# Retention attention in chunks of 64 positions, with the two batches of a pair in the two halves of the partitions

## The chip, the core and the metric

The kernel runs on one core of a Trainium2 chip. The core has a matrix engine (TensorE, "PE" in the profile, with its loads of the stationary operand counted apart as "PEld"), three engines for elementwise work (VectorE "DVE", ScalarE "ACT", GpSimd "POOL") and a fifth, SyncE "SP", that here only starts transfers. Each engine works through its own list of instructions in order. SP, ACT and POOL start DMA transfers from their lists too, and such an instruction stands in the engine's queue like any other. TensorE writes to PSUM, which has eight banks of 512 f32 in each of the 128 partitions; DVE and ACT read PSUM, POOL does not.

The metric is the device time of the program in microseconds, the median of several runs. A change of more than about 0.2% can be told from none.

## The reference

A retention layer without softmax feeds a multiplicative feed-forward layer. With 8 batches, 8 heads, 576 positions and 64 values per head, all f32:

```python
scores = q @ k.T / sqrt(64)                # per batch and head, 576 x 576
rel    = pos[:, None] - pos[None, :]
Dmat   = where(rel >= 0, gamma[h] ** rel, 0)
x      = (scores * Dmat) @ v               # put back as 4608 tokens x 512
a, b   = x @ w1, x @ w2                    # each 4608 x 1024
out    = (a * b @ w3) @ w_out              # 4608 x 512
```

The weights come as 64-bit floats and are turned into f32 on the chip.

## The kernel before

**Attention.** `gamma ** rel` is split: q is multiplied by `gamma ** pos` and v by `gamma ** -pos`, so the mask is only a triangle of ones. The sequence of a pair of batches is cut into five chunks, the first of 64 positions and four of 128; a pair and a chunk are one group g, 20 in all (`NC` = 5 chunks, `G` = 20; groups 0, 5, 10 and 15 are the short ones). Positions lie in the partitions of the loaded tiles `ld_k`, `ld_q`, `ld_v`, with 16 batch-and-head columns of 64 values beside one another. For each group there are four stages on TensorE, each with 16 small matmuls (every f32 matmul shows as two loads and two matmuls in the profile, so that a stage is 32 of each):

- `score` (L233): k times q, contracted over 64 values, a 128 by 128 result. Two of them stand in the array at once, in its two row halves. The results fill four PSUM banks `sc`, and four DVE multiplications by the mask (L236) write them to `pm`.
- `state` (L255): k times v, contracted over 128 positions, added up over the chunks in one PSUM bank `st`. Two at once, in the two column halves. ACT copies the sum to `sb` (L259).
- `pv_state` (L274): the state before the chunk times q. Contraction and output are both 64 wide: four at once, one in each quarter of the array.
- `pv` (L299): `pm` times v, contracted over 128 positions, two at once in the column halves, added to the same two banks `xps`; ACT copies them to `xT` (L306).

q and k must stand with the 64 values in the partitions before `score`. In some groups PE transposes them (`front`, L218, copied by ACT at L221), in others they are loaded in blocks of 32 by 32 (`load_blocks`, L171, 16 transfers a tile on SP's queue) and transposed by DVE (L190). v is scaled by POOL or DVE (L204), or by eight ACT instructions, one a head for both batches (L202).

**Feed-forward.** The large products use Strassen's scheme. Up to about 157 us `up` (L524) multiplies tokens by w1 and w2 while DVE and ACT convert the weights; up to 212 us w3 is multiplied by w_out (L477); then `down` (L637), and from 363 us on `up2` (L1028), a second form with seven steps a half. One `up2` step is seven products of four matmuls (0.65 us each): p1, p5, the product left over from the step before, then one onto a bank that ACT first filled with p1 (`seed`, L1047), then three more. Its weights come back from DRAM into a ring of three places (`ra`, L939 on POOL's queue).

**Order.** The order of all instructions is written out by hand. In the last part the loop over groups runs some `up2` and `down` steps by `work(n)`, then `pv(g)` with its copies, then the load of v for group g+2 (L93, on POOL's queue), `state(g+1)` and `score(g+1)`. The load of v waits until `pv(g)` has read the buffer. The ACT scaling of that v is put into the list `beside` and is issued in two halves in the first two `up2` steps after it (L1058); where the group has only `down` steps, it is issued after them, just before `pv`. The transposes of the next q and k on DVE are put into `aside`, in the last two steps before `pv`.

**Banks.** All results but `st` and the two `seed` banks are allotted in turn from a pool `acc`, of seven banks up to 335 us and of five from then on (L925): each new tile takes the bank used longest ago and waits until that one has been read. In the last part these are p1 and p5 of every `up2` step, five results of every `down`, and `xps` (two) and `sc` (four) of each group.

Of the kernel before, what the change touches and what calls it, by code (L numbers as in the profile page):

```python
# [8 lines left out]
F32 = mybir.dt.float32  # L9
# [10 lines left out]
def kernel(  # L20
# [31 lines left out]
    G = NB2 * NC  # L52
    NB = 3
# [27 lines left out]
    acc = acc_part.enter_context(tc.tile_pool(name="acc", bufs=7, space=PSUM))  # L81
# [5 lines left out]
    def load(g, names, engine=nc.sync):  # L87
        i, c = divmod(g, NC)
        sz = sizes[c]
        src = {"k": k, "q": q, "v": v}  # L90
        for nm in names:
            t = pools["ld"].tile([P, 2 * H, D], F32, tag="ld_" + nm, name="ld_" + nm)
            engine.dma_start(  # L93
                t[:sz], src[nm][2 * i:2 * i + 2, :, starts[c]:starts[c] + sz, :].rearrange("b h p d -> p (b h) d"))
            live[nm, g] = t

    dq = ffn.tile([P, 4, 2, TB], F32, tag="c", name="dq", bufs=1).rearrange("p a b s -> p (a b s)")[:H, :S]
    nc.scalar.dma_start(dq, decay_q)
# [8 lines left out]
                            base=0, pattern=[[1, P]], channel_multiplier=-1)  # L107

# [3 lines left out]
    gk = const.tile([P, NC, H], F32, tag="gk", name="gk")  # L112
    gq = const.tile([P, NC, H], F32, tag="gq", name="gq")
    gqs = const.tile([P, NP, S // 32], F32, tag="gqs", name="gqs")
    nc.scalar.dma_start(gk[:short, 0, :], decay_k[:short, :])
    nc.scalar.dma_start(gk[:, 1:, :], decay_k[short:, :].rearrange("(c p) h -> p c h", p=P))
# [3 lines left out]
    gps = acc.tile([P, NC, H], F32, tag="acc", name="gps")  # L120
    for c in range(NC):
        nc.tensor.transpose(gps[:sizes[c], c, :], dq[:, starts[c]:starts[c] + sizes[c]], ident[:H, :H])
    for c in (0, slice(1, NC)):
        n = short if c == 0 else P
        nc.vector.tensor_copy(gq[:n, c, :], gps[:n, c, :])
# [69 lines left out]
    def scale(g, nm, scalar=False, engine=nc.gpsimd):  # L195
        c = g % NC
        sz = sizes[c]
        t, gam = live[nm, g], {"q": gq, "v": gk}[nm]
        t = t[:sz].rearrange("p (b h) d -> p b h d", b=2)
        if scalar:  # L200
            for h in range(H) if scalar is True else scalar:
                nc.scalar.mul(t[:, :, h, :], t[:, :, h, :], gam[:sz, c, h:h + 1])  # L202
            return
        engine.tensor_tensor(  # L204
            out=t, in0=t, in1=gam[:sz, c].unsqueeze(1).unsqueeze(3).to_broadcast([sz, 2, H, D]), op=ALU.mult)

    def front(g, names="kq"):
        c = g % NC
        sz = sizes[c]
        for nm in names:  # L210
# [3 lines left out]
            for b in range(2):  # L214
                tp = acc.tile([P, NP, P], F32, tag="acc", name="tp")
                for p in range(NP):
                    h = b * H + 2 * p
                    nc.tensor.transpose(tp[:, p, :sz],  # L218
                                        src[:sz, h:h + 2, :].rearrange("p a d -> p (a d)"),
                                        ident[:sz, :sz])  # L220
                nc.scalar.copy(dst[:, b, :, :sz], tp[:, :, :sz])  # L221
            live[nm + "T", g] = dst

    def score(g):
        c = g % NC
        sz = sizes[c]
        kT, qT = live["kT", g], live["qT", g]
        pm = pools["fr"].tile([P, 2, 2, NP, P], F32, tag="pm", name="pm", bufs=1)
        for b in range(2):
            sc = [acc.tile([P, NP, P], F32, tag="acc", name="sc") for j in range(2)]  # L230
            for p in range(NP):
                for j, hs in enumerate(heads):
                    nc.tensor.matmul(sc[j][:sz, p, :sz], kT[hs, b, p, :sz], qT[hs, b, p, :sz],  # L233
                                     start=True, stop=True)
            for j in range(2):
                nc.vector.tensor_mul(pm[:sz, b, j, :, :sz], sc[j][:sz, :, :sz],  # L236
                                     mask[:sz, :sz].unsqueeze(1).to_broadcast([sz, NP, sz]))
        live["pm", g] = pm

    def state(g):  # L240
        c = g % NC
        sz = sizes[c]
        if c == NC - 1:
            return
        vs = live["v", g]
        kn = live["k", g]
        if c == 0:
            live["st"] = st_ps.tile([P, 2, NP, D], F32, tag="st", name="st")
        st = live["st"]

        for b in range(2):
            for p in range(NP):
                for j, hs in enumerate(heads):
                    h = b * H + 2 * p + j
                    nc.tensor.matmul(st[hs, b, p, :], kn[:sz, h, :], vs[:sz, h, :],  # L255
                                     start=(c == 0 and b == 0 and p == 0), stop=(c == NC - 2),
                                     skip_group_check=True)
        sb = pools["fr"].tile([P, 2, NP, D], F32, tag="sb", name="sb")
        nc.scalar.copy(sb, st)  # L259
        live["sb", g + 1] = sb  # L260

    bank_order = [(b, n) for b in range(2) for n in range(2)]

    def pv_state(g):

        sz = sizes[g % NC]
        qT = live["qT", g]

        banks = live["xps", g] = [acc.tile([P, 2, 2, P], F32, tag="acc", name="xps") for r in range(2)]
        if g % NC:  # L270
            for m, (b, n) in enumerate(bank_order):
                for r, j in ((0, 0), (0, 1), (1, 0), (1, 1)):
                    p = 2 * r + n
                    nc.tensor.matmul(banks[r][heads[j ^ r], b, n, :sz], live["sb", g][heads[j], b, p, :],  # L274
                                     qT[heads[j], b, p, :sz], start=(m == 0), stop=False,
                                     skip_group_check=True)

    def pv(g):
# [16 lines left out]
        for m, (b, n) in enumerate(bank_order):  # L295
            for r in range(2):
                for half in range(2):
                    p, j = 2 * r + n, half ^ r
                    nc.tensor.matmul(banks[r][heads[half], b, n, :sz], vs[:sz, b * H + 2 * p + j, :],  # L299
                                     pm[:sz, b, j, p, :sz], start=(c == 0 and m == 0), stop=True,  # L300
                                     skip_group_check=True)
# [425 lines left out]
    state(0)  # L727
# [14 lines left out]
    pv_state(1)  # L742
    convert_up_to(3)
    convert(2)
    state(1)
# [19 lines left out]
    state(2)  # L765
# [5 lines left out]
    copies = pv(2)  # L771
# [4 lines left out]
    state(3)  # L776
# [8 lines left out]
    pv(3)()  # L785
# [4 lines left out]
    owed.append(2)  # L790
    pv(4)()
# [129 lines left out]
    def open_second():  # L921
# [3 lines left out]
        acc = ctx.enter_context(tc.tile_pool(name="acc", bufs=5, space=PSUM, reuse_waits="tile"))  # L925
# [198 lines left out]
    state(NC)  # L1124
# [4 lines left out]
    for g in first_pair:  # L1129
# [21 lines left out]
        pv(g)()  # L1151
        load(g + 2, "v", nc.scalar if in_blocks[g + 2] else nc.sync)
        if in_blocks[g + 2] and (g + 2) % NC != NC - 1:
            load(g + 2, "k")
        state(g + 1)
        score(g + 1)
# [35 lines left out]
    state(g)  # L1192
# [3 lines left out]
    for g in range(2 * NC, G):  # L1196
# [27 lines left out]
        pv(g)()  # L1224
# [3 lines left out]
        if g + 2 < G:  # L1228
            load(g + 2, "v", nc.gpsimd)
            if (g + 2) % NC != NC - 1:  # L1230
                loads.append(lambda g=g: load(g + 2, "k", nc.gpsimd))
        if g + 1 < G:
            state(g + 1)
            score(g + 1)
# [49 lines left out]
```

## Time and profile before

| | |
|---|---|
| median of 3 runs | 858.88 us (858.45 to 860.29) |
| the profiled execution | 850.68 us, its span 848.9 us |
| mean granted TensorE clock | 0.989 |
| PE busy | 819.3 us (97%), 6085 matmuls |
| DVE, POOL, ACT busy | 541.2, 325.6, 283.2 us |
| DMA | 126.96 MB, mean 150 GB/s |

The groups' attention falls into three stretches: 0 to 83 us (groups 0 to 4), 231 to 340 us (5 to 9) and 385 to 706 us (10 to 19; the score of group 10 is at 364 us). Their mean busy times, by the view of windows:

| stretch, us | PE | DVE | ACT | POOL | DMA share | GB/s |
|---|---|---|---|---|---|---|
| 0 to 83 | 73.81 | 64.88 | 58.27 | 6.64 | 0.93 | 195 |
| 231 to 340 | 107.31 | 63.31 | 15.27 | 33.05 | 0.61 | 150 |
| 385 to 706 | 315.24 | 197.62 | 101.62 | 185.58 | 0.62 | 167 |

A line of the profile names the kernel's line, the engine, what is written and what is read; "x32" is a count of instructions, and "<-" ahead of a time in brackets names what ended the engine's wait. In the chain of waits each piece has its start, its length and what it was. Times of one profiled execution are all measured from its first instruction.

### The profile page before, as it was taken

The numbers are of one execution on the slowest core, as the hardware profiler recorded it, in microseconds if no ns is written. First come the engines' busy times: TensorE is split into PE (matmuls) and PEld (weight loads), VectorE is DVE, ScalarE is ACT, GpSimd is POOL, SyncE is SP. The second block draws the span as 40 slices with busy tenths as digits, with TensorE's granted clock in tenths as the row PEclk, the third lists the DMA queues.
The fourth block names the chain that finished last, engine by engine and source line by source line (L and its number), as shares of the span: only waits on it lengthen the run. The fifth ranks groups of instructions, "written<-read, shape, count | busy, mean of one in ns | idle before, by whom it ended". The sixth has DMA issues, their size and how long they took to land.

```text
span 848.9 us, 15774 instructions
## 1 busy us (share of the span) xinstructions
PE 819.3 (97%) x6085; PEld 738.1 (87%) x6085; DVE 541.2 (64%) x887; ACT 283.2 (33%) x581; POOL 325.6 (38%) x330
## 2 busy tenths in 40 slices
PE   7899999999999999979998999999999999999998
PEld 6889999644989998869998889998899998899987
DVE  4899999991644477615657644759735768446653
ACT  4777556670111101033343024342034331033300
POOL 1100010001104181395545935556916468445500
PEclk8999999999999999999999999999999999999999
DMA  9995454436046487979786147787275452245401
GB/s 193 217 224 128 77 150 125 126 98 112 1 98 125 75 220 251 307 209 220 190 229 167 44 93 228 201 238 177 58 156 183 140 208 69 77 148 189 159 25 51
DMA packets 201291, 126.96 MB, mean 150 GB/s; under 512 B 161272, under 2 KB 183032, under 8 KB 201216
## 3 DMA queue, kind: packets, MB, share of 16 engines
q1 hardware_dynamic: 170944, 50.14, 29.1%
q0 software_dynamic: 11776, 63.71, 23.0%
q10 hardware_dynamic: 18496, 12.10, 5.3%
q8 instruction: 48, 0.79, 0.4%
q14 instruction: 27, 0.22, 0.1%
HBM read 103.62 MB, written 22.28 MB: 148 GB/s over the span
## 4 chain that ended last, share of the span: by engine, by line
PE 79%; DMA 7%; DVE 7%; issue 3%; SPq 2%; ACT 1%; POOL 0%; ACTq 0%; DVEq 0%; POOLq 0%
PE po L637 24%; PE up L1028 15%; PE up L524 13%; PE seed L1028 11%; PE ps L477 6%; DMA ld_v<-in_v_dram 3%; PE xps L299 3%; PE sc L233 3%; DMA ra<-kept 2%; PE xps L274 1%; SPq L171 1%; DVE c L529 1%; DVE ab L1003 1%; DMA bl_q<-in_q_dram 1%; PE st L255 1%
## 5 line engine op out<-in xcount | busy, mean ns | idle before, releaser
L637 PE MATMUL po<-w3o,ab 128*128 128x256 f32 x552 | 125.0, 381 | 1.4 <-DVE ot L641 0.5
L637 PEld LDWEIGHTS po<-w3o,ab 128*128 128x128 f32 x552 | 103.9, 190 | 17.4 <-DVE ot L641 1.2
L1033 POOL TENSOR_TENSOR cc<-cc 128x384 f32<-128x384 f32 x112 | 109.3, 1001 | 4.1 <-ACT cc L1051 2.4
L1040 DVE TENSOR_TENSOR cc<-seed,cc 128x384 f32<-128x384 f32 x88 | 48.7, 553 | 72.9 <-PE seed L1028 68.5
L181 POOL TENSOR_TENSOR bl_q<-bl_q,gqs 128x512 f32<-128x512 f32 (+1 forms) x30 | 30.8, 1048 | 127.7 <-DMA bl_q<-in_q_dram 91.8
L939 POOL DMA_DIRECT2D ra<-kept x54 | 30.6, 567 | 124.1 <-PE seed L1028 103.3
L1028 PE MATMUL up<-xT,ra 128*128 128x192 f32 x384 | 74.2, 330 | 0.6 <-DMA ra<-kept 0.6
L1040 DVE TENSOR_TENSOR cc<-up,cc 128x384 f32<-128x384 f32 x88 | 48.4, 550 | 36.8 <-PE up L1028 31.5
L524 PE MATMUL up<-xT,wA 128*128 128x192 f32 x384 | 70.4, 327 | 0.0
L529 DVE TENSOR_TENSOR c<-up,c 128x384 f32<-128x384 f32 x80 | 44.0, 550 | 38.9 <-PE up L524 38.3
L1028 PEld LDWEIGHTS up<-xT,ra 128*128 128x128 f32 x384 | 64.4, 192 | 2.0 <-DMA ra<-kept 0.9
L236 DVE TENSOR_TENSOR pm<-sc,mask 128x512 f32<-128x512 f32 (+1 forms) x80 | 45.4, 626 | 32.1 <-PE sc L233 32.0
L637 PE MATMUL po<-wB,forms 128*128 128x256 f32 x288 | 65.2, 379 | 0.5 <-DVE forms L611 0.5
L524 PEld LDWEIGHTS up<-xT,wA 128*128 128x128 f32 x384 | 63.4, 190 | 1.1 <-issue 0.5
L637 PEld LDWEIGHTS po<-wB,forms 128*128 128x128 f32 x288 | 54.6, 190 | 8.2 <-PE po L637 0.8
L1047 ACT COPY seed<-up 128x384 f32<-128x384 f32 x56 | 25.9, 463 | 100.1 <-PE up L1028 46.6
L1028 PE MATMUL seed<-e,ra 128*128 128x192 f32 x256 | 52.9, 337 | 5.2 <-DVE cc L1040 2.9
L1028 PE MATMUL up<-ra 128*128 128x192 f32 x288 | 55.1, 328 | 1.9 <-DMA ra<-kept 1.9
L477 PE MATMUL ps<-wo,w3T 128*128 128x512 f32 x128 | 55.1, 592 | 0.0
L204 POOL TENSOR_TENSOR ld_v<-ld_v,gk 128x1024 f32<-128x1024 f32 (+1 forms) x9 | 17.1, 1899 | 90.5 <-DMA ld_v<-in_v_dram 90.5
L679 DVE TENSOR_TENSOR ab<-ab,forms 128x512 f32<-128x512 f32 x17 | 17.1, 1008 | 53.3 <-PE po L637 53.3
L1028 PEld LDWEIGHTS seed<-e,ra 128*128 128x128 f32 x256 | 43.7, 194 | 7.8 <-DVE cc L1040 3.6
(127 smaller groups left out, 1597.2 us busy)
## 6 DMA issues: line engine op xcount, KB each, us to landing
ra<-kept POOLq DMA_DIRECT2D x54, 896.0 KB, 5.0
raw<-in_moe_w_dram SPq DMA_DIRECT2D x72, 128.0 KB, 3.0
bl_q<-in_q_dram SPq DMA_DIRECT2D x216, 32.0 KB, 3.2
out_dram<-ot ACTq DMA_DIRECT2D x54, 128.0 KB, 2.3
bl_k<-in_k_dram SPq DMA_DIRECT2D x136, 32.0 KB, 2.4
raw<-in_moe_w_dram SPq DMA_DIRECT2D x16, 256.0 KB, 6.0
ld_k<-in_k_dram SPq DMA_DIRECT2D x8, 512.0 KB, 5.9
raw<-in_moe_w_out_dram SPq DMA_DIRECT2D x32, 128.0 KB, 2.7
```

Of the source, the lines that this page charges most:

```text
L181: nc.gpsimd.tensor_tensor(out=part, in0=part, in1=gqs[:, :, n0:n0 + n].unsqueeze(3).to_broadcast([P, NP, n, BL]), op=ALU.mult)
L233: nc.tensor.matmul(sc[j][:sz, p, :sz], kT[hs, b, p, :sz], qT[hs, b, p, :sz], start=True, stop=True)
L236: nc.vector.tensor_mul(pm[:sz, b, j, :, :sz], sc[j][:sz, :, :sz], mask[:sz, :sz].unsqueeze(1).to_broadcast([sz, NP, sz]))
L477: nc.tensor.matmul(ps, live["w3T", ft][:, g, :], live["wo"][:, g, :], start=(g == 0), stop=(g == KF - 1))
L524: nc.tensor.matmul(ps[:, w, :], a[:, w, r, :], b[:, r, :], start=(new and w == r == 0), stop=(w == r == 1), skip_group_check=True)
L529: nc.vector.tensor_add(c[:, to], ps, c[:, sb])
L637: nc.tensor.matmul(ps[nm], a[A][:, f, :], live["W"][B][:, f, :], start=(f == 0 and not on), stop=(f == NP - 1), skip_group_check=True)
L939: engine.dma_start(ring[n % 3], kept[n % 14 // 7][nm])
L1028: nc.tensor.matmul(ps[:, w, :], weight_of(slot, a, w), B[b], start=(new and w == 0), stop=True, skip_group_check=True)
L1033: nc.gpsimd.tensor_tensor(out=o, in0=o, in1=i, op=ALU.add)
L1040: nc.vector.tensor_add(c[:, j], ps, with_add[:, j])
L1047: nc.scalar.copy(p6, p1)
```

## The change

A chunk of 64 positions takes the place of the 128, but a group keeps its 64 or 128 positions: it has one or two chunks (`chunks(g)`), and a loaded tile now holds batch 0 of the pair in partitions 0 to 63 and batch 1 in 64 to 127, with a chunk index s, 8 heads and 64 values in the free dimension. Every matmul of the four stages has 64 rows, 64 columns and 64 moving columns, and four of them stand in the four quarters of the array.

- `score`: 32 matmuls a full group into two `sc` banks, two mask multiplications in place of four; `pm` has two buffers of half the size.
- `state(g, s)`: 16 matmuls and one ACT copy for each chunk; `st` takes two banks, so `acc` has six and later four.
- `pv_state`: 16 matmuls a chunk, with the state of that chunk.
- `pv`: in two halves (`second`); between them ACT reads one column of a bank into `hand`, and the second half waits for that. Callers pass work to be put between the halves: `state(g, 1)` and `score(g + 1)`, which ran after `pv` before.
- `load`: two transfers a chunk (one a batch), four in place of one for a full group; in the last chunk of a pair k is loaded for the first 64 positions, as `state(g, 0)` needs them.
- `scale` on ACT: one instruction a head and chunk, 16 in place of 8 for a full group.

The core of it:

```diff
-    acc = acc_part.enter_context(tc.tile_pool(name="acc", bufs=7, space=PSUM))
+    acc = acc_part.enter_context(tc.tile_pool(name="acc", bufs=6, space=PSUM))
...
-            t = pools["ld"].tile([P, 2 * H, D], F32, tag="ld_" + nm, name="ld_" + nm)
-            engine.dma_start(
-                t[:sz], src[nm][2 * i:2 * i + 2, :, starts[c]:starts[c] + sz, :].rearrange("b h p d -> p (b h) d"))
+            t = pools["ld"].tile([P, 2, H, D], F32, tag="ld_" + nm, name="ld_" + nm)
+            for s in range(n):
+                s0 = starts[c] + s * CS
+                for b in range(2):
+                    engine.dma_start(t[heads[b], s], src[nm][2 * i + b, :, s0:s0 + CS, :].rearrange("h p d -> p h d"))
...
             for h in range(H) if scalar is True else scalar:
-                nc.scalar.mul(t[:, :, h, :], t[:, :, h, :], gam[:sz, c, h:h + 1])
+                for s in range(n):
+                    nc.scalar.mul(t[:, s, h, :], t[:, s, h, :], gam[:, n0 + s, h:h + 1])
...
+        sc = [acc.tile([P, 2, NP, CS], F32, tag="acc", name="sc") for j in range(2)]
+        for s in range(n):
+            at_s = slice(s * CS, (s + 1) * CS)
             for p in range(NP):
+                for b in range(2):
+                    for j, hs in enumerate(heads):
+                        nc.tensor.matmul(sc[j][heads[b], s, p, :], kT[hs, b, p, at_s], qT[hs, b, p, at_s],
+                                         start=True, stop=True)
...
+        for p in range(NP):
+            for b, rows in enumerate(heads):
                 for j, hs in enumerate(heads):
+                    h = 2 * p + j
+                    nc.tensor.matmul(st[hs, b, p, :], kn[rows, s, h, :], vs[rows, s, h, :],
+                                     start=(g % NC == 0 and p == 0), stop=at_end, skip_group_check=True)
...
+        for second in range(2):
+            if second:
+                nc.scalar.copy(hand[heads[0]], banks[1][heads[0], 1, 1, sz - 1:sz])
+                for work_between in fill:
+                    work_between()
+            for s in range(chunks(g)):
+                for n in range(2):
+                    for b, half in ((0, 0), (1, 1), (0, 1), (1, 0)):
+                        r = b ^ half ^ second
+                        p, j = 2 * r + n, half ^ r
+                        nc.tensor.matmul(
+                            banks[r][heads[half], b, n, s * CS:(s + 1) * CS], vs[heads[b], s, 2 * p + j, :],
+                            pm[heads[b], j, s, p, :], start=(c == 0 and not second and n == 0), stop=True,
+                            skip_group_check=True)
...
-        acc = ctx.enter_context(tc.tile_pool(name="acc", bufs=5, space=PSUM, reuse_waits="tile"))
+        acc = ctx.enter_context(tc.tile_pool(name="acc", bufs=4, space=PSUM, reuse_waits="tile"))
...
-        pv(g)()
+        if g + 1 < G:
+            pv(g, lambda: state(g, 1), lambda: score(g + 1))()
+        else:
+            pv(g)()
...
-            state(g + 1)
-            score(g + 1)
+            state(g + 1, 0)
```

Groups 0, 1, 4, 9 and 19 have nothing between the halves of `pv`; groups 2 and 3 have `state(g, 1)` alone. The tables of decays are laid out by 64 positions, which takes one more transfer of q's decays.

## The prediction

> **What bounds the kernel now.** The page first:
>
> ```profile
> span 848.9 us, 15774 instructions
> PE 819.3 (97%) x6085; PEld 738.1 (87%) x6085; DVE 541.2 (64%) x887; ACT 283.2 (33%) x581; POOL 325.6 (38%) x330
> PE 79%; DMA 7%; DVE 7%; issue 3%; SPq 2%; ACT 1%; POOL 0%; ACTq 0%; DVEq 0%; POOLq 0%
> ```
>
> PE is the bound: the chain lies on it for 79% of the span. So the first question is what the four stages cost it, which the chain of waits shows in one late group (11):
>
> ```profile
> 414.01 1.03 PE xps L274 x32
> 415.05 1.90 PE xps L299 x32
> 416.94 0.93 PE st L255 x32
> 417.88 1.99 PE sc L233 x32
> 419.86 1.50 PE up L1028 x8
> ```
>
> 5.85 us a full group. L274 has four matmuls at once (8 turns of 0.129), L299 two of the same 128 columns (16 turns of 0.119), L255 two of 64 columns (16 turns of 0.058). So four at once cost a turn no more than two, and half the columns halve it.
>
> The second question is what stands ready to take PE's place. ACT's and POOL's timelines behind the same group:
>
> ```profile
> 416.77 1.07 ACT L306 COPY xT<-xps 128x512 f32<-128x512 f32 x2 [4.12 <-PE xps L299]
> 417.92 0.59 ACT L259 COPY sb<-st 128x512 f32<-128x512 f32 x1
> 423.69 1.28 ACT L202 ACTIVATE ld_v<-ld_v,gk 128x128 f32<-128x128 f32 x4 [0.47 <-DMA ld_v<-in_v_dram]
> 424.88 0.46 ACT L1042 COPY cc<-up 128x384 f32<-128x384 f32 x1
> 425.29 0.46 ACT L1047 COPY seed<-up 128x384 f32<-128x384 f32 x1
> ...
> 417.87 1.21 POOL L93 DMA_DIRECT2D ld_v<-in_v_dram  x1 [3.62 <-PE xps L299]
> ```
>
> The load of v starts when `pv` has ended (416.78) and lands 5.8 us later. ACT waits for it, scales, and only then fills the bank (L1047) for a product of the next step, which PE reaches at 426.39: 0.6 spare. Behind group 14 nothing is spare, and the chain leaves PE altogether:
>
> ```profile
> 508.70 6.37 DMA ld_v<-in_v_dram
> 515.10 0.92 ACT ld_v L202 x3
> 516.28 0.46 ACT cc L1042
> 516.74 0.39 ACT seed L1047
> 517.17 0.92 PE seed L1028 x4
> ```
>
> Third, how late DVE is when a group starts (group 18, PE there at 664.2):
>
> ```profile
> 662.23 2.74 DVE L1003 TENSOR_TENSOR ab<-cc 128x384 f32<-128x384 f32 x1
> 664.90 1.23 DVE L190 STREAM_TRANSPOSE kT<-bl_k 128x1024 f32<-128x1024 f32 x1
> 666.97 0.54 DVE L1040 TENSOR_TENSOR cc<-up,cc 128x384 f32<-128x384 f32 x1
> 667.89 0.53 DVE L1040 TENSOR_TENSOR cc<-up,cc 128x384 f32<-128x384 f32 x1
> ```
>
> The last two free the banks of p1 and p5, at 667.5 and 668.4. With five `acc` banks the first `sc` tile has a free bank; with four, the two `sc` tiles need just these two.
>
> **The change part by part.**
>
> *The array.* Each stage of a full group becomes 16 turns of four matmuls of 64 columns: at 0.058, 0.93 us. Four stages 3.73, and 0.2 for entering the mode once (1.03 against 8 turns of 0.109 shows 0.16): 3.9 against 5.85, 1.9 us saved. Over 16 full groups, and some 1.1 in the four short ones, about 35 us of PE time. The turn isn't in the trace: bounded below by 0.058 (L255), above by 0.129 (L274, were its 128 columns no part of the price), which makes 8.25 a group. I take 0.058, as both halvings have a row.
>
> [...]
>
> *What PE meets after the stages.* The next product takes the first `xps` bank, whose copy (0.59) starts when `pv` ends, with only `state(g+1, 0)` (0.47) between: 0.3 lost. So 1.6 of the 1.9 at best, work starting 4.25 after the group's start in place of 5.85.
>
> *`hand`.* The copy is tiny, but PE's whole queue stands behind it. Group 11 has 1.4 us of fill, which covers a copy and two semaphores (0.5, L306's row starts 0.1 after its matmul). Without cover (groups 0, 1, 4, 9, 19) it costs 0.5. It stands in ACT's queue behind the scaling: in group 17 that runs 626.06 to 628.51 as eight, so to about 630.0 as sixteen.
>
> *ACT's scaling.* Sixteen of 64 for eight of 128. L202 takes 0.295 (four in 1.28); copies of 256 and 512 (0.37, 0.59) give 0.84 ns an element, so 0.24 each and a batch of eight 2.0 in place of 1.28: 0.75 later.
>
> *The load of v.* `pv` now ends with `state(g, 1)` and `score(g + 1)` inside it: at start + 3.4 in place of 2.85, 0.55 later. Four transfers for one: POOL's short load takes 0.86, so issue is at most 3.4 in place of 1.21 (+2.2); a short load lands 4.5 after issue against 6.4 (down to -1.5). I take the landing as unchanged, between the two. So L1047 is 0.55 + 0.75 = 1.3 later than before, and PE, 1.6 earlier, waits for it: the gain is gone, and 1.3 less the spare time is lost.
>
> *Four banks.* Where DVE is late (groups 13, 15, 16, 18), `score(g + 1)`, now in the middle of `pv`, waits for p5's bank or kT, and `pv`, `xT` and the load of v behind it.
>
> *DVE* loses 40 of 80 mask multiplications (about 0.62: 25 us), beside PE; nothing on the path, as what makes it late stands ahead of them. *Second state copies*: 16 x 0.59 on ACT, read a group later; nothing, with ACT at 33%; 0.6 each if ACT were late. *k of last chunks*: four loads of 256 KB beside 0.62 DMA share; nothing. *k loads on POOL*: up to +2.2 us of issue in each of six groups, ahead of POOL's ring loads and L1033; up to 1 each if DVE waits for these (it spends 5.4 us waiting for L1033 now); nothing taken. *More instructions to fetch*: nothing, PE's loads and matmuls doubled in these stages only. *`acc` at six*: `up` needs a bank back after 2.6 us, ACT returns it in time; nothing.
>
> **By stretch** (+ is time won):
>
> 0 to 83 us (DMA share 0.93, ACT 58 of 83): the chain runs through loads and their issues on SP, where a blocked issue takes 2.66 and 6.59 us, which absorbs most of some 40 more issues; PE's savings don't count, and in group 1 the `hand` copy stands behind the conversion's ACT work. -1.0 (from -5 to +3).
>
> 231 to 340 us: ACT and POOL are light. Group 5 +0.5 and +2.0; group 6 nothing, since kT for group 8 waits for SP's 33 issues (266.8 to 285.9), counted from the transposes of group 7; group 7 +1.8; group 8 +0.9 (no state before); group 9 +0.3. Sum +5.5 (from +2 to +8).
>
> 385 to 706 us, by the terms above:
> - 10: kT's copy (391.2) holds `score`, `pv` ends 0.95 later, 0.75 for ACT, 0.5 spare, 0.2 of the wait hidden: -1.0.
> - 11: -1.3 + 0.6, so -0.6. 12: ACT, not the load, led there, with 1 spare: 0.
> - 13: kT at 465.2 as before; the left-over product now comes after `score`, and its three DVE multiplications hold the next `down`: -1.0.
> - 14: `pv` ends 0.2 later, 0.75 for ACT, nothing spare: -1.0.
> - 15: `score` waits until 547.1, so `pv` ends at 548.4 in place of 543.9: v lands at 555.2, L1047 done at 558.1 in place of 554.2; -3.4, of which the 0.8 us that PE now waits at 561.8 for `ra` is taken up: -2.8.
> - 16: `score` waits until 585.5, the left-over product comes 2.5 later, its multiplications hold `down`: -0.7.
> - 17: `hand` waits for the scaling, `pv` ends 2.1 later, 0.75 for ACT: between -1.6 and -2.9; -2.0.
> - 18: `score` at 668.5, work at 670.9 in place of 669.8: -1.1.
> - 19: +0.3.
>
> Sum -9.9. In all -1.0 + 5.5 - 9.9 = -5.4. The profiled execution's 850.7 (span 848.9 and 1.8 around it) would become 856.1. It lies 8.2 under the median, so the forecast against the median is 858.9 + 5.4, 864.
>
> **Rivals.**
>
> *The gain is kept.* If the four smaller loads land about 1.5 us sooner (the short load's row), ACT is no longer late behind 10, 11, 12, 14 and 17: +1.5, +1.6, +1.6, +1.1, +1.6, with 0.3 for 19 and nothing for the late-DVE groups, +7.7; with +5.5 and 0 at the start, 13.2 faster: 845. For it: the short load's row. Against it: POOL must issue four. It decides the sign when more than about 1 us of landing is won in each.
>
> *Issue binds.* The four issues on POOL take 3.4, and the last part lands 2 us later; behind 10, 11, 12, 14, 15 and 17 that goes straight into the chain, 6 x 2.0: 876. For it: the 0.86 row; against it: parts move while others are issued.
>
> *The turns don't shrink.* At 0.129 a group costs 8.25 + 0.2: 2.4 x 16 = 38 us more, 897. For it: no row has four at once with 64 columns. Against it: both halvings in the rows.
>
> **How the numbers follow.** The main case 0.50, gain kept 0.28, issue 0.13, turns 0.09. The main case's own range is 858 to 871, from the ends of its stretches (-5 + 2 - 13 to +3 + 8 - 8, pulled in since they don't fall together). Leaving out the turns (0.09) and the lower part of the kept gain (0.10) gives 845 to 877. No change (within 0.2%, 1.7 us, what a measurement here can tell): 0.10, from between the main case and the kept gain; faster 0.30; slower 0.60, the rest.
>
> **What would show it.** Each stage at 0.93 for 64 matmuls in the chain (over 1.5: the turns). L202 in batches of eight near 2.0, starting on the DMA, and PE's first `seed` product of the second `up2` step waiting about 2 us for L1047, in groups 10, 11, 14, 15, 17. PE waiting in `score` for L1040 or kT in 13, 15, 16, 18. `pv`'s second half in 17 waiting for ACT. In the middle stretch PE time falls by about 8 and the end moves by about 5. The prediction is wrong if L202 finds v there (then it is faster), or if the ring loads on POOL come late (then slower).

## The result and the profile after

The changed kernel takes 915.69 us against 858.66 us: 1.066 times as long, with an interval of 1.057 to 1.074. Measured once more beside later experiments it was 1.073 times (1.062 to 1.084). The forecast was 864 us, with 877 as the upper end: the sign was right, and some 50 us were missing. The profiled execution took 916.36 us. Runs of one and the same kernel spread more than the 0.2% named at the start: those of the kernel before went from 846 to 860 us beside the experiments, so the intervals are what a difference is to be judged by.

The page of the changed kernel, the lines that answer to those of before, and the row of the queue that brings instructions (blocks, MB, share of the 16 DMA engines; it had 48 blocks before):

```profile
span 914.6 us, 20159 instructions
PE 811.1 (89%) x8121; PEld 727.3 (80%) x8121; DVE 536.7 (59%) x847; ACT 309.9 (34%) x709; POOL 345.5 (38%) x372
q8 instruction: 64, 1.05, 0.5%
PE 60%; DMA 13%; DVE 9%; SPq 5%; issue 5%; POOL 4%; ACT 4%; ACTq 0%; DVEq 0%; POOLq 0%
```

TensorE is no longer the whole story: its share of the chain fell from 79% to 60%, and everything else on the chain grew. Two sums over the starts of all matmuls say by how much. A matmul's own time is taken as the time to the next start, but no more than its columns need; the rest is waiting. Own time fell from 788.1 to 764.1 us, waiting rose from 55.6 to 145.4 us; -24.0 and +89.8 make the +65.7 of the two spans.

Not all of this waiting is standing still. The mean granted clock of TensorE fell from 0.989 to 0.963. By the view of windows it was 0.50 from 448.8 to 452.2 us, at the end of the stop shown below and behind it, and from 500.0 to 503.4 us, behind a wait of 4.4 us for `kT`, where the 64 matmuls of `score` took 1.99 us in place of 0.93. If what was withheld always came as a half, as it did there, the two means amount to 68 us at half speed in place of 19. By the same sums, matmuls that took up to twice their time in such stretches make about 13 of the 89.8 us (an estimate). This comes behind the waits; no experiment here takes it apart from them.

Group 11 shows the gain and its end. The chain of waits (start, length, what):

```profile
443.52 1.09 PE xps L282 x64
444.61 0.47 PE xps L315 x32
445.07 0.47 PE st L261 x32
445.54 0.93 PE sc L237 x64
446.48 0.11 PE xps L315 x6
446.58 2.43 issue
449.02 1.01 PE xps L315 x25
```

Here the stages are as fast as forecast: 64 matmuls in 0.93 to 1.09 us. Then, in the middle of `pv`'s second half, TensorE stands still for 2.43 us, and the profile names nothing that it waits for. The stop alone is more than the 1.9 us that the group was to win. The waits of TensorE over the whole span (us in total, times, longest) have more of that kind, and others:

```profile
PE seed L1048 <- ACT seed L1067: 9.7, 5, 5.4
PE xps L315 <- ACT hand L307: 9.7, 8, 2.7
PE po L654 <- DVE forms L628: 8.6, 2, 7.1
...
PE sc L237 <- issue: 7.6, 2, 5.1
PE sc L237 <- DVE cc L1060: 7.3, 6, 2.9
PE xps L315 <- issue: 4.9, 3, 2.4
...
PE sc L237 <- DVE kT L198: 4.4, 1, 4.4
PE st L261 <- issue: 4.1, 3, 1.9
```

Before, the row with the most had 3.0 us in all.

Where the time was lost is seen by comparing when the same product of `up` or `up2` runs. How much later than before it is, in us, in the profiled executions of the changed kernel and of some of the experiments below:

```
product, at us in the kernel before     91.8  283.7  315.7  399.6  455.1  529.0  649.3  759.1
the changed kernel                      17.7   17.8   19.5   27.7   34.7   49.6   57.8   65.8
changed, order of before                18.0   17.6   15.9   22.9   27.5   30.4   34.5   40.4
before, loads in four                    4.9    4.5    4.1   12.9   15.0   15.3   15.2   19.2
before, loads, banks, scaling            8.6    8.3    8.2   17.9   19.9   21.4   24.9   29.6
```

### The profile page after: what moved, and what is told of

Its sections match the earlier page's. It is cut to its first block, busy times and chain, and to the rows that moved or that the text cites. A ratio compares the mean times of both kernels' runs of the same rounds, so it can differ in the third digit from the quotient of the medians.

```text
span 914.6 us, 20159 instructions
## 1 busy us (share of the span) xinstructions
PE 811.1 (89%) x8121; PEld 727.3 (80%) x8121; DVE 536.7 (59%) x847; ACT 309.9 (34%) x709; POOL 345.5 (38%) x372
## 4 chain that ended last, share of the span: by engine, by line
PE 60%; DMA 13%; DVE 9%; SPq 5%; issue 5%; POOL 4%; ACT 4%; ACTq 0%; DVEq 0%; POOLq 0%
PE po L654 18%; PE up L1048 12%; PE seed L1048 10%; PE up L541 10%; PE ps L494 6%; DMA ld_v<-in_v_dram 4%; SPq L179 3%; DMA kept<-wA 2%; DVE ab L1023 2%; DMA out_dram<-ot 2%; DMA bl_q<-in_q_dram 2%; DVE cc L1060 1%; DMA ld_q<-in_q_dram 1%; ACT ld_v L209 1%; PE sc L237 1%
## 5 line engine op out<-in xcount | busy, mean ns | idle before, releaser
L1048 PE MATMUL up<-xT,ra 128*128 128x192 f32 x384 | 76.5, 337 | 0.1
L654 PE MATMUL po<-wB,forms 128*128 128x256 f32 x288 | 67.1, 387 | 8.7 <-DVE forms L628 8.6
L1048 PE MATMUL seed<-e,ra 128*128 128x192 f32 x256 | 55.3, 346 | 17.1 <-ACT seed L1067 9.5
L654 PEld LDWEIGHTS po<-wB,forms 128*128 128x128 f32 x288 | 55.6, 194 | 17.7 <-issue 9.3
L1048 PEld LDWEIGHTS up<-xT,ra 128*128 128x128 f32 x384 | 66.7, 198 | 1.0 <-DVE pm L240 0.2
L1023 DVE TENSOR_TENSOR ab<-cc 128x384 f32<-128x384 f32 x64 | 66.1, 1067 | 0.0
L1048 PEld LDWEIGHTS up<-ra 128*128 128x128 f32 x288 | 49.3, 194 | 0.9 <-PE seed L1048 0.8
L658 DVE TENSOR_TENSOR ot<-po,ot 128x256 f32<-128x256 f32 x72 | 30.3, 421 | 32.5 <-PE po L654 31.9
```

What stands on the lines that cost most here:

```text
L654: nc.tensor.matmul(ps[nm], a[A][:, f, :], live["W"][B][:, f, :], start=(f == 0 and not on), stop=(f == NP - 1), skip_group_check=True)
L658: nc.vector.tensor_add(ot[:, to[0], to[1]], ps[nm], ot[:, sb[0], sb[1]])
L1023: nc.vector.tensor_mul(ab, v[:, :, 0, :], v[:, :, 1, :])
L1048: nc.tensor.matmul(ps[:, w, :], weight_of(slot, a, w), B[b], start=(new and w == 0), stop=True, skip_group_check=True)
```

## The experiments

**Does TensorE run out of instructions?** In the group above, some 390 instructions had run at 7.8 ns each when it stopped, and a 16 KB block of instructions began to move at 446.33 us, just ahead of the stop. 64 such blocks brought the 16,242 matmuls and weight loads of this profile, 48 the 12,170 of the kernel before: some 254 a block, and the stops below come at every 256. The first experiment is a program of matmuls alone, with nothing to wait for. `rest(40)` is 40 matmuls of 128 by 128 with 512 columns, `four(96, 64)` goes 96 times round the four quarters with 64 columns, 1536 instructions:

```diff
+    rest(40)
+    four(96, 64)
+    rest(40)
+    four(96, 128)
+    rest(40)
+    four(96, 192)
...
```

> A program of TensorE matmuls alone, nothing else computed (attention and FFN are left out): 1536 instructions of four-quarter turns at 64 columns, then as many at 128 and at 192 columns, each after a long rest on wide matmuls; then three bursts of 256 and three of 512 instructions with 8 us of wide matmuls between; then the 1536 at 64 columns again while 16 MB are being loaded. Theory 1 (PE runs out of fetched instructions): the first two blocks of 256 go at 7.3 ns an instruction, then PE stops at each block and the pace is that of the fetches, one block in about 3.6 us, 14 ns an instruction: 18 us in place of 11.2 for the first segment, 21 to 22 us at 128 columns (13.6 ns an instruction of its own), no stops at 192 columns (31 us) and none in the bursts of 256. Beside the loads the blocks come later still. Theory 2 (the stops of the changed kernel are waits for other engines that the profile does not name): there is nothing to wait for here, and the first segment takes 11.2 us without a stop.

Its chain of waits, the segment with 64 columns, and the one line of that with 128:

```profile
38.91 4.11 PE b L81 x269
43.02 1.58 issue
44.60 2.09 PE b L81 x128
46.69 1.36 issue
48.05 2.09 PE b L81 x128
50.15 1.36 issue
51.51 2.09 PE b L81 x128
53.60 1.36 issue
54.96 1.96 PE b L81 x115
```

```profile
91.45 21.12 PE b L81 x768
```

The stops come after every 128 matmuls, that is 256 instructions (a load and a matmul each), and a period is 3.45 us: 13.5 ns an instruction, while TensorE uses them up at 7.3. The first stop came after 269 matmuls, 538 instructions. The segment took 17.9 us from its first to its last start, and the one with 128 columns, whose own pace is 13.6 ns an instruction, ran without a stop in 20.9; so did that with 192 columns (31.1). In the bursts of 256 there was no stop; of the three bursts of 512 two had one, of 1.25 us. With 16 MB of loads started ahead of the last segment it had stops again, of 1.6 to 1.85 us, 20.0 us in all. But the loads had gone through by then (they ran in the first 44 us, beside the head of the first segment), so this is no test of a busy DMA. No other engine works beside these segments, the granted clock is 1.00 in all of them, and the stops come at every 256 instructions: theory 1 is shown, with a pace, and neither theory 2 nor a slower clock can explain these stops.

**Does it cost as much inside the kernel?** Two twins of the kernel before, with the same 3.7 us of idle array time ahead of `pv` in 14 groups, once as 512 instructions, once as 68:

```diff
+    def pad():
+        t = [acc.tile([P, P], F32, tag="acc", name="idle") for r in range(2)]
+        for _ in range(32):
+            for r, j in ((0, 0), (0, 1), (1, 0), (1, 1)):
+                nc.tensor.matmul(t[r][heads[j ^ r], :D], ident[heads[j], :D], ident[heads[j], :D],
+                                 start=True, stop=True)
...
+        pad()
         pv(g)()
```

and in the wide twin, in place of the loop:

```diff
+        for n in range(17):
+            nc.tensor.matmul(t[n % 2], ident, ident, start=True, stop=True)
```

> The kernel before with 512 instructions of idle four-quarter turns (64 columns) ahead of each pv in groups 5 to 8 and 10 to 19: 3.7 us of array time each, 52 us in all, nothing read from them. Theory 1: a stop of 1.6 to 2.7 us in or behind each as well, so 20 to 36 us more than its wide twin. Theory 2: no more than the wide twin.

> The twin: the same 3.7 us of array time as 17 idle matmuls of 128 columns, 68 instructions, at the same 14 places. Both theories: 35 to 55 us slower than before, no stop that names nothing.

958.67 us (1.124, 1.114 to 1.134) against 902.27 us (1.057, 1.050 to 1.064): the dense twin is 56 us slower, more than the 20 to 36 expected of the stops. One of its places in the chain of waits:

```profile
447.77 3.54 PE idle L139 x232
451.32 2.26 issue
453.58 0.52 PE idle L139 x18
```

Its trace has 19 such stops, 38 us in all, of 0.9 to 4.2 us each; the wide twin and the kernel before have none. The other 18 us between the twins are not accounted for. In the changed kernel eight stops of this kind (nothing named by the profile, over 110 matmuls in the 2.5 us before) make 20 us. Six of them are longer (2.1 to 2.7 us, and 5.28 in the start) than in the program that moves nothing else (1.6 to 1.85). By the view of windows the DMA engines were fully busy in the longest (a share of 1.07 from 76.7 to 79.4 us), and 2% busy around one of 1.5 us at 728 us. Whether a busy DMA makes the stops longer was not tried by itself.

**Is it the number of instructions, or how densely they stand?** The kernel before with each matmul of 128 columns in three stages as two of 64 (shown for `score`; in `pv_state` and `pv` the two column halves are the outer loop):

```diff
-                    nc.tensor.matmul(sc[j][:sz, p, :sz], kT[hs, b, p, :sz], qT[hs, b, p, :sz],
-                                     start=True, stop=True)
+                    for x0 in range(0, sz, P // 2):
+                        at_x = slice(x0, x0 + P // 2)
+                        nc.tensor.matmul(sc[j][:sz, p, at_x], kT[hs, b, p, :sz], qT[hs, b, p, at_x],
+                                         start=True, stop=True)
...
```

> The kernel before with each matmul of 128 columns in the score, state-product and value stages as two of 64: same array time (16 turns of 0.119 become 32 of 0.058), same loads and waits, 448 instructions a full group in place of 256 (12.7 ns each). Theory 1 at 14 ns an instruction and two blocks of lead: 0 to +0.6 us a group, 859 to 868 us. [...]

879.76 us, 1.032 (1.025 to 1.040): more than the 859 to 868 of theory 1. Its chain of waits:

```profile
426.90 1.09 PE xps L278 x64
427.99 2.02 PE xps L304 x64
430.01 0.93 PE st L257 x32
430.94 3.77 PE sc L235 x64
```

Twice the instructions cost `pv_state` and `pv` 0.06 and 0.22 us (1.03 and 1.80 before), and no stop without a name occurs anywhere. Only `score` doubled, from 1.99 to 3.77, and that is the edit's own doing: its inner loop sets both pieces of a matmul on the same row half of the array, one behind the other, where the two row halves took turns before. In the trace of before the two matmuls of such a pair start 7 ns apart, and a pair comes every 0.112 us; now a matmul of 64 columns takes 0.059 us, as long as a pair of that width in `state` (0.058), as if they ran one at a time. At 1.78 us a full group, 16 groups make the 28 us. So twice the instructions, at 8.5 and 15.8 ns each in these two stages and 17 ns over the group, are as good as free. With `score` stretched, the group was not as dense as planned, so the 0 to 0.6 us a group were not tried.

**Fewer instructions in the changed kernel.** `pv_state`'s products left out of the result, in the changed kernel and in the kernel before:

```diff
-        if g % NC:
+        if False:
             for s in some:
```

> The changed kernel without the products of the state with q (they are left out of the result; all else stays). A full group has 384 instructions in its stages in place of 512. Theory 1 (instruction fetch): the stops of 2 to 2.7 us behind groups 5 to 17 go or shrink below 0.7, so far more is won than the 0.98 us a group that the products take: 870 us or less. Theory 2 (loads of v, scaling, banks): those waits stay, at most the 14 x 0.98 are won, and some of that is lost to waits: 900 to 910 us.

> The control: the kernel before without the products of the state with q (left out of the result). Both theories: it has no stops, so at most 14 x 1.03 us is won: 844 to 855 us.

902.19 us (1.056, 1.047 to 1.065) and 849.20 us (0.994, 0.989 to 0.998). The changed kernel won 1.0 to 1.7% by it, not the 5% that theory 1 was to give; the time lies where the rival was to put it (900 to 910). For theory 1 the expectation had the size of a run wrong: it took 512 instructions to be in hand when a group starts. The first stop came after 538 in the program, but after some 390 in group 11 of the changed kernel, and with runs of 384 groups 11 and 12 stop again, for 2.2 and 2.1 us. Four such stops remain in the trace, 10 us in all, so this experiment doesn't tell the theories apart.

**The other parts, one at a time on the kernel before.** Loads in four, banks, scaling, and the three together:

```diff
-            engine.dma_start(
-                t[:sz], src[nm][2 * i:2 * i + 2, :, starts[c]:starts[c] + sz, :].rearrange("b h p d -> p (b h) d"))
+            for s0 in range(0, sz, P // 2):
+                for b in range(2):
+                    engine.dma_start(
+                        t[s0:s0 + P // 2, b * H:(b + 1) * H],
+                        src[nm][2 * i + b, :, starts[c] + s0:starts[c] + s0 + P // 2, :].rearrange("h p d -> p h d"))
```

> The kernel before with one part of the change: each load of v, k and q as four transfers (two halves of the positions by two batches), layout and all else unchanged. The prediction's own step (parts move while others are issued, landing unchanged): within 3 us of before. Issue binds (0.6 us more on the queue for each extra transfer, v landing 2 us later behind six late groups, SP's and the start's loads later): 10 to 18 us slower. The shorter loads land sooner: 3 to 8 us faster.

```diff
-    acc = acc_part.enter_context(tc.tile_pool(name="acc", bufs=7, space=PSUM))
+    acc = acc_part.enter_context(tc.tile_pool(name="acc", bufs=6, space=PSUM))
...
-        acc = ctx.enter_context(tc.tile_pool(name="acc", bufs=5, space=PSUM, reuse_waits="tile"))
+        acc = ctx.enter_context(tc.tile_pool(name="acc", bufs=4, space=PSUM, reuse_waits="tile"))
```

> The kernel before with one part of the change: six and four acc banks in place of seven and five. If the banks alone are what holds the score stage (four sc tiles a group here, two in the changed kernel, so this bounds it from above): 4 to 12 us slower, in the groups where VectorE is late. If they cost only together with the new order: within 3 us.

```diff
-                nc.scalar.mul(t[:, :, h, :], t[:, :, h, :], gam[:sz, c, h:h + 1])
+                for b in range(2):
+                    nc.scalar.mul(t[:, b, h, :], t[:, b, h, :], gam[:sz, c, h:h + 1])
```

> The kernel before with one part of the change: ScalarE scales v in sixteen pieces of 64 columns in place of eight of 128. The prediction's step: a batch of eight pieces 0.75 us longer, on the path behind groups 10, 11, 14 and 17 and in the start, less some spare time: 2 to 6 us slower; nothing if ScalarE has slack.

> The kernel before with the loads in four, six and four banks and the scaling in sixteen together: all of the change but the four-quarter stages and their order. If the three add up (18.8 + 7 + 3.5): 3.3% over before, about 882. If they cover one another: 870 to 876. What the changed kernel with score behind the loads (5.0% over before) has beyond this is what the four-quarter stages come to with their stops, against the 35 us that the prediction had them win.

| on the kernel before | ratio to before | interval |
|---|---|---|
| loads in four | 1.022 | 1.015 to 1.029 |
| six and four banks | 1.008 | 1.005 to 1.012 |
| scaling in sixteen | 1.004 | 1.000 to 1.008 |
| all three | 1.042 | 1.032 to 1.052 |

They add up (3.4% one by one, 4.2% together, within the interval). The loads cost the 10 to 18 us of "issue binds", but not where that was expected: by the table of products above they lose 4.9 us by 92 us, 9 more between 316 and 400 us, where SP's queue also moves the weights, only 2.3 from there to 649 us, with groups 11 to 17, and 4 at the end. The case was the start and the weights, not GpSimd. Which of the waits in these two places carries it was not taken apart.

**The order.** The changed kernel with the order of before, and then with only `state(g, 1)` between `pv`'s halves:

```diff
-            pv(g, lambda: state(g, 1), lambda: score(g + 1))()
+            pv(g)()
+            state(g, 1)
...
             state(g + 1, 0)
+            score(g + 1)
```

> The changed kernel with the order of before: the stages of pv and state of one group together, state and score of the next group behind the loads, nothing between pv's two halves. Theory 3 (the new order costs: score stands in pv's middle, so pv, the copies and the load of v wait with it, and the left-over products come after it, their multiplications beside GpSimd's sums at 3.4 us each in place of 0.5): 8 to 20 us faster than the changed kernel, some 895 to 908, although the hand copy is now uncovered (0.5 us a group). Theory 1 alone (instruction fetch): the same instructions stand as densely, so no gain, and 5 to 8 us slower for the uncovered hand.

```diff
-            pv(g, lambda: state(g, 1), lambda: score(g + 1))()
+            pv(g, lambda: state(g, 1))()
...
             state(g + 1, 0)
+            score(g + 1)
```

> The changed kernel with only state(g, 1) between pv's two halves; score of the next group back behind the loads, as before. If score in pv's middle is what the new order costs (its wait for VectorE holds pv, and the left-over multiplications come beside GpSimd's sums), this keeps what the full return to the old order won and also covers the hand copy (0.43 us in 14 groups): 884 to 892. If any work in pv's middle costs as much, 905 to 917.

894.50 us (1.049, 1.044 to 1.056) and 895.79 us (1.050, 1.042 to 1.058). The order costs 14 to 20 us, and within the intervals all of that is `score` in `pv`'s middle. Whether the hand copy is covered can't be told from the times: uncovered it stops TensorE for some 0.43 us in about ten places and longer in others (15.1 us in 19 waits, against 9.7 in eight in the changed kernel), and not all of that reaches the end. The largest piece is in group 13. The chain of waits of the changed kernel, and GpSimd's timeline beside it:

```profile
500.36 1.99 PE sc L237 x64
502.35 0.85 PE xps L315 x32
503.20 0.98 PE seed L1048 x4
...
504.76 10.12 DVE ab L1023 x3
```

```profile
504.95 1.88 POOL L189 TENSOR_TENSOR bl_q<-bl_q,gqs 128x256 f32<-128x256 f32 x2
506.81 1.94 POOL L968 TENSOR_TENSOR xT<-xT 128x384 f32<-128x384 f32 x2
508.71 1.93 POOL L968 TENSOR_TENSOR ra<-xT 128x384 f32<-128x384 f32 x2
```

and VectorE's timeline in the old order:

```profile
494.49 1.48 DVE L1023 TENSOR_TENSOR ab<-cc 128x384 f32<-128x384 f32 x3
495.88 1.28 DVE L240 TENSOR_TENSOR pm<-sc,mask 128x512 f32<-128x512 f32 x2
```

The same three multiplications take 10.12 us beside GpSimd's sums and 1.48 before them. Over the trace of the changed kernel, all 44 that met no GpSimd sum took 0.55 us; the 20 that met one took 0.8 to 8.6, 2.2 in the mean. (Before: 49 at 0.55, 15 at 1.6 in the mean.) A program of the two engines alone was to try it (`multiply` and `from_bank` are VectorE's, the first from SBUF to SBUF, the second with a PSUM bank as one input; `sums` are GpSimd's):

```diff
+    multiply(10)
+    from_bank(10)
+    nc.gpsimd.tensor_copy(y[:, :1], ab[9][:, 0, :1])
+    sums(40)
+    multiply(10)
+    nc.gpsimd.tensor_copy(y[:, :1], ab[9][:, 0, :1])
+    sums(20)
+    from_bank(10)
...
```

> VectorE and GpSimd alone (attention and FFN are left out): ten multiplications of 128x384 from SBUF to SBUF as the kernel has them, ten sums of a PSUM bank with SBUF, first alone, then each beside a row of GpSimd sums of 128x384. If GpSimd's sums slow VectorE's multiplications: 0.49 us each alone, 2.5 to 3.5 beside them, and the sums from the bank 0.5 in both places. If the 3.4 us in the changed kernel came from something else (DMA, a wait): 0.5 throughout.

Of the second ten multiplications only the last, at 35.42 us, was still running when the sums began, at 35.47, so that half of it tried next to nothing. A copy of one column by GpSimd, in the way by chance, shows a wait on the other side (the timelines of POOL and DVE):

```profile
31.28 4.11 POOL L90 COPY y<-ab 128x1 f32<-128x1 f32 x1 [30.13 <-DVE ab L82]
```

```profile
31.05 4.93 DVE L78 TENSOR_TENSOR ab<-x 128x384 f32<-128x384 f32 x10
```

The copy, 0.18 us elsewhere in the program, ended at 35.39, when nine of the ten multiplications were through; the tenth writes what the copy reads and came after it. The ten sums from a bank beside GpSimd's sums took 0.47 each from start to start, as without them. So it was the copy that lost time beside multiplications with both inputs in SBUF, 4.11 us in place of 0.18, and the ten sums that read a bank lost none. For the multiplication held up by GpSimd's sums the kernels' traces alone speak.

**Spreading the stages, other queues, the start.** Three tries to win something back, and a mix. The first two stand on the changed kernel in the order of before, the third on the changed kernel itself; the mix has state alone in the middle, the loads on SP and the table in one piece.

```diff
-            work(tail)
+            apart = tail if g not in ready else 0
+            work(tail - apart)
...
+            work(apart)
             state(g + 1, 0)
             score(g + 1)
```

> The changed kernel in the order of before, and in the groups that have a fourth step of the FFN (11, 12, 15, 18; not those that end a group of tokens) that step stands between pv and the next group's state and score, so that the stages come as two runs of 256 instructions with 9 us of wide products between. Theory 1: the stops of 1.4 to 1.9 us in these groups' stages go, 4 x 1.5 = 6 us faster than the same order without it, 885 to 890 us. If the stops are waits for other engines, they stay or move: within 2 us of the same order without it, or slower, since the load and the state of the next group come apart.

```diff
-            load(g + 2, "v", nc.gpsimd)
+            load(g + 2, "v")
...
-            loads.append(lambda g=g: load(g + 2, "k", nc.gpsimd, 1 if (g + 2) % NC == NC - 1 else 2))
+            loads.append(lambda g=g: load(g + 2, "k", nc.sync, 1 if (g + 2) % NC == NC - 1 else 2))
```

> The changed kernel in the order of before, with the late groups' loads of v and k issued by SP in place of GpSimd. Theory 4 (eight issues a group at 0.6 to 0.7 us stand in GpSimd's queue ahead of its ring loads and its sums, for which VectorE and then TensorE wait): 4 to 12 us faster than with GpSimd (894), so 882 to 890. If GpSimd's queue has slack, or SP's own issues come as late: 891 to 898.

```diff
-    for b in range(2):
-        nc.scalar.dma_start(dq[:, :, b, :], decay_q.rearrange("h (c p) -> h c p", p=CS))
+    nc.scalar.dma_start(dq, decay_q)
...
-        nc.tensor.transpose(gps[:, c, :], dq[:, c].rearrange("h b p -> h (b p)"), ident[:H, :H])
+        for b in range(2):
+            nc.tensor.matmul(gps[heads[b], c, :], dq[:, c * CS:(c + 1) * CS], ident[:H, :H], start=True, stop=True)
```

> The changed kernel with the decay table loaded in one piece as before, and brought to both halves by matmuls, in place of two loads of 256 B pieces that take 3.6 us at the head of the chain. If the head decides: 3 to 5 us faster than the changed kernel, 912. If the first loads of q and k land no sooner, or later waits take it up: within 2 us of it.

> The three together (state alone in pv's middle, loads on SP, decay table in one piece). If they add up: 872 to 884. What then remains over before is instruction fetch, the loads in four and the scaling in sixteen: it stays slower than before (852).

| on the changed kernel | ratio to before | interval |
|---|---|---|
| spread, order of before | 1.045 | 1.037 to 1.053 |
| loads on SP, order of before | 1.076 | 1.068 to 1.085 |
| decay table in one piece | 1.072 | 1.063 to 1.080 |
| state in the middle, loads on SP, table in one piece | 1.073 | 1.063 to 1.082 |

The spread order can't be told from the plain one (1.049). Five of the unnamed stops remain in its trace, as many as in the plain order, four of them before 340 us, where nothing was spread. In its group 11 the loads now start earlier and follow one another on GpSimd, ahead of the sums that VectorE and TensorE need:

```profile
448.06 0.80 POOL ld_k L101 x2
...
449.42 1.36 POOL ld_k L101 x2
...
450.80 1.96 POOL cc L1053 x2
...
452.79 0.57 DVE cc L1060
```

That is theory 4's chain, but the remedy was worse. On SP's timeline the eight issues stand ahead of the next group's blocks, of which sixteen take 12.46 us:

```profile
448.45 2.66 SPq L101 DMA_DIRECT2D ld_v<-in_v_dram  x4
451.15 3.20 SPq L101 DMA_DIRECT2D ld_k<-in_k_dram  x4
454.46 12.46 SPq L179 DMA_DIRECT2D bl_q<-in_q_dram  x16
```

The table in one piece wins nothing that can be told (the changed kernel has 1.066 and 1.073); that later waits of the start take it up is likely, but not shown. The mix shows the loads on SP and nothing else. No version here beats the kernel before.

## Why the prediction was wrong

The runs split the loss. Loads, banks and scaling cost 4.2% on the kernel before. The four-quarter stages, with all that came with them, were to win 4% and cost 0.7% more. The new order costs another 1.6 to 2.3%. By the table of products the start lost 17.7 us, where 1.0 was forecast; from there to 316 us it lost 1.8, where 5.5 were to be won by 340; from 316 to 400 us 8.2, where nothing was taken; and the late groups lost 38, where 9.9 was forecast.

*More instructions to fetch: nothing.* This is the main step that failed. The stops, 20 us, are nearly as much as the whole gain of TensorE's own time. Twice the instructions were as good as free in two stages of the kernel before, at 8.5 and 15.8 ns each. In the changed kernel halving a turn's columns doubled the density as well, to 7.3 ns in `score`, and a block's supply came at 13.5 ns in the program of matmuls alone. The prediction gave the supply no pace. The densest stage of before, L255 with 14.5 ns an instruction, ran for 64 instructions; the change made runs of 512.

*The array.* Right in kind: each stage in 0.93 to 1.09 us. TensorE's own time fell by 24 us, not 35; the term was sized from the sums of a full group, and by the same sums `score` and `pv` won about 14 us each, and `state` and `pv_state` lost 3 together, as the last chunk of a pair now has a state of its own. From all three other parts (1.042) to the changed kernel in the old order (1.049) there is no gain left: the stages, with their stops, the slower clock behind waits and the `hand` and state copies, come to about +0.7%, with an uncertainty of about 1.2%, in place of -4%. How much of that is the stops alone was tried in the twins, not in the changed kernel.

*The loads.* The landing was held to be unchanged, from 2.2 later to 1.5 sooner. That held in the late groups: in group 11 the first of the four is issued at 450.43 and the last lands at 455.92, 5.5 us, against 5.8 before (the 5.8 count from the issue at 417.87, not from the end of `pv`). Of the seven full loads on GpSimd six are within 0.8 us of before, and one takes 9.3 in place of 6.4. What was missing lies elsewhere, and it is the second step that failed: the start, whose SP waits were said to absorb the issues (they don't: +4.9), and the weights' stretch, which was given no term (+8.8).

*Four banks, scaling.* Right. `score` waits for p5 (7.3 us in six places) and kT; eight scalings take 2.02 us by ScalarE's timeline, where 2.0 was forecast. On the kernel before they cost 0.8% and 0.4%.

*Group 13's multiplications: -1.0.* This is the third: the whole order was given some 6 us (groups 13, 15, 16 and 18) and cost 14 to 20. The mechanism was right, the size wrong: at 0.5 us each the multiplications would have cost 1.5, but behind `score` they fell beside GpSimd's sums and took 10.12. That this happens stood in the trace of before: 2.74 us for one of them in group 18. The prediction quoted that row as VectorE's lateness and did not ask what made it five times as long.

*`hand`: 0.5 without cover.* Too low in the start, where ScalarE is late: of the 9.7 us of waits for it, three there take 1.0 to 2.7 each.

*Second state copies: nothing.* Wrong in the start. The chain of waits of the changed kernel there:

```profile
94.75 0.67 PE st L261 x32
...
95.86 0.68 ACT e L412
...
98.05 0.48 ACT sb L264
```

The copy stands in ScalarE's queue behind three conversions, and `pv_state` waits 2.9 us for it; "ACT at 33%" was a mean over the span, and the start has 58 of 83 us.

*The rivals.* "Issue binds" had its price nearly right and its place wrong, so the price was luck; "the turns don't shrink" (897) was nearest in time, and false. No rival had TensorE stop for its own instructions.

## What to carry to other kernels

Before a stage is cut into smaller matmuls, count instructions over time: here a block of 256 took 3.45 us, 13.5 ns an instruction, and runs at 7.3 to 7.8 ns came to a stop, after 538 instructions in the program and after some 390 in group 11, though the stages themselves were as fast as forecast. And before work is moved across engines or in time, look what GpSimd is doing then: here multiplications of VectorE with both inputs in SBUF, 0.55 us each without GpSimd's sums, took up to 8.6 beside them.

## What the hardware did that was not expected

- In the program of matmuls alone a block of 256 TensorE instructions came every 3.45 us, 13.5 ns an instruction; TensorE used them at 7.3 ns in four-quarter turns of 64 columns. The stops (1.36 us there, 2.43 in group 11) have no releaser in the profile and show as "issue", mostly between two matmuls of the same line.
- VectorE's multiplications of 128x384 from SBUF took 0.55 us without, and up to 8.6 us beside GpSimd's sums, which run in a row; GpSimd's copy of one column took 4.11 in place of 0.18 us beside ten of them. The longest, 8.6 us from 506.29 us on, spans eight of GpSimd's sums of 0.98 us each and ended 0.4 us after the last of them.
- `score`, each matmul cut in two with both pieces one behind the other on the same row half of the array, took 3.77 in place of 1.99 us for the same columns.
- Behind waits of 2.4 and 4.4 us TensorE was granted half its clock for 3.4 us each; behind the second `score` took 1.99 in place of 0.93 us.
